# A start in another order: attention and a channel mix on one TensorE

## The chip, the core and the metric

The program runs on one core of a Trainium2 chip. A core has TensorE (PE: matmuls, with a separate queue of weight loads, PEld), VectorE (DVE), ScalarE (ACT), GpSimd (POOL) and SyncE (SP), which issues the transfers here; each works through its own instructions in a fixed order and waits at semaphores for the others. The metric is the device time of one execution in microseconds (us). Another execution, taken by the hardware profiler, left the profile and the trace that are read below.

## The reference

Attention with pooled keys and values, then a channel mix on its output, in float32; the three weights reach the program in 64 bits:

```python
# q, k, v: [8, 8, 576, 64];  w_k: [512, 1024], w_v: [1024, 512], w_r: [512, 512]
k_p = k.reshape(B, H, 72, 8, D).mean(axis=3)      # v_p likewise
scores = scale * np.matmul(q, k_p.transpose(0, 1, 3, 2))
attn = np.exp(scores - np.max(scores, axis=-1, keepdims=True))
attn = attn / (np.sum(attn, axis=-1, keepdims=True) + 1e-09)
x = np.matmul(attn, v_p)                          # then [B, S, H * D] = [8, 576, 512]
x_prev = ...                                      # x, one token later, 0 at a batch's first
xk = mu_k * x + (1.0 - mu_k) * x_prev
xr = mu_r * x + (1.0 - mu_r) * x_prev
k = np.maximum(xk @ w_k, 0.0)
v = k * k @ w_v
return 1.0 / (1.0 + np.exp(-(xr @ w_r))) * v
```

## The kernel before, in words

**Tiles and stages.** The 8 x 576 tokens are 36 tiles of 128 and 12 chunks of 384. A tile has its scores (L524, all heads, 576 columns in a pair of PSUM banks `sc`), its softmax on VectorE and ScalarE (maximum L535, `e` L542 or L549 and after, sum L556, 1/sum L559 and L562), the division by the sum (`px` L566 for the last 8 keys, `pm` L572 for the first 64) and transposes (`pth` L589, of `pm`; `pr` copies L618 and L620, L622, and their transposes L628). A chunk has four attention products (L671, into `bank`), their mix with the token before (L678 on ScalarE, small copies through `carry` L687 and L689 on GpSimd, L696 on VectorE), eight hidden groups (`x_k @ w_k`, L740, then relu and square, `sh`), three gates (L789) and three mixing groups (L821). Chunk 0 works in full float32, where one matmul of the program is two records of PE in the trace. Later chunks split each operand in a high and a low fp32r part (`xkh`, `xkl`, `sh`, `sl`, `w_k` high and low, by L408 and L411) and take three matmuls of such parts for one.

**Sums and weights.** The pooled sum over 8 rows of k (`keys`), v (`values`) and of v's last 8 keys (`last_values`) goes for batches 0 and 1 through PE, as eight matmuls with the identity (L429, `SUMMED_ON_PE`); for later ones it is three halvings (L418), k's on VectorE, v's on GpSimd. k0 to k3, v0 to v3, r0 and r1 are the parts of the first two batches. Each of the 20 weight blocks is turned from 64-bit to float32 words by `convert`: |x| on ScalarE, then four VectorE instructions (L374, L376, L381, L386) through one of two places `tmp`; `split` makes the two parts when chunk 0 has used the block, the low one on VectorE or GpSimd by the table `LOW_BY`.

**What sets the order.** Nothing is reordered at run time. A planner, `Order`, writes the program: each piece of work is a generator that yields what it needs (`need`), the place it takes (`take`) or the next instruction with its engine and estimated length; pieces have a due time (`order.add(due, ...)`, from `FIRST`, `PER_TOKEN`, `tile_due`), and the planner hands out instructions by due times, estimated lengths and the estimated delay between engines (`LATENCY`). Its results are one fixed order per engine. `LOADS` is the order of the first transfers on SP's queue; `stage` has three places for raw k and v, `qs` two for q, `sc` one pair of banks, `bank` and `mm` three banks each. `BY_HEAD` names the tiles whose exponentials are eight small ScalarE instructions with the sum beside them, `COPIES_ON_ACT` the number of tiles whose `pr` copies are on ScalarE.

Of the kernel before, what the change touches and what calls it, by code (L numbers as in the profile page):

```python
# [173 lines left out]
def attention_then_channel_mix(  # L174
# [122 lines left out]
    def load_constants():  # L297
        yield "sp", 0.6, False
        nc.sync.dma_start(out=mask_sb, in_=mask)
        order.fetched("mask", 2)  # L300
        yield "sp", 0.6, False
        nc.sync.dma_start(out=mu_sb, in_=mu)
        order.fetched("mu", 2)
# [614 lines left out]
```

## Time and profile before

| what | us |
|---|---|
| median of 3 runs (660.5 to 662.31) | 661.78 |
| the profiled execution | 657.92 |
| its span in the trace | 656.1 |
| first attention product begins | 33.46 |
| first hidden matmul of chunk 1 begins | 109.86 |
| first gate matmul of chunk 1 begins | 134.31 |
| last mixing matmul ends | 652.05 |

All times in rows of the trace are us from the start of the span. The four moments in the middle cut the span in stages: the first sums and softmaxes; chunk 0's products, hidden groups, gates and mixing groups, with the conversion of all weights; chunk 1's hidden groups; and the other chunks. In a row of the timeline stand the start, the duration, the engine, the line of the kernel, the operation, out<-in with its shape, and, in brackets, the idle time before it and what ended that; "x8" behind a row is eight instructions of one group in a row. In a row of groups stand the busy time in all, the mean of one in ns, and the idle time before them. In a row of windows stand a stretch and its length, and for each engine the busy time and the instructions.

### The profile page before, as it was taken

How to read it: one execution, taken by the hardware profiler on the slowest of the kernel's cores; microseconds unless marked ns; L12 is line 12 of the kernel's file. 1: busy time of each engine (PE TensorE's matmuls, PEld its weight loads, DVE VectorE, ACT ScalarE, POOL GpSimd, SP SyncE). 2: the span in 40 equal slices, each digit the busy share in tenths (PEclk: the TensorE clock that was granted, in tenths of full speed). 3: DMA queues.
4: the chain of work that ended last, by engine and by line, in shares of the span. 5: the costliest groups of instructions: out<-in, count | busy, mean ns of one | idle time of the engine just before them, and what ended most of it. 6: DMA issues, size and time to landing. Idle time of an engine off the chain costs nothing.

```text
span 656.1 us, 9196 instructions
## 1 busy us (share of the span) xinstructions
PE 631.1 (96%) x3328; PEld 546.8 (83%) x3328; DVE 415.8 (63%) x797; ACT 335.7 (51%) x713; POOL 211.9 (32%) x329
## 2 busy tenths in 40 slices
PE   6699989899999999999999999999999999999997
PEld 6555646888988988988978998998988998998986
DVE  2789966885776667854884657754784654653421
ACT  3766447575456455554464446455365445454420
POOL 1211036636147017505344206604443303302200
PEclk9989999999999999999999999999999999999999
DMA  7893014012240115101411105101321101000001
GB/s 255 279 378 145 0 49 151 2 50 71 93 133 33 48 43 183 33 26 39 169 40 49 33 16 199 43 17 48 139 71 40 42 17 32 33 1 29 20 1 48
DMA packets 34989, 50.93 MB, mean 78 GB/s; under 512 B 6528, under 2 KB 22912, under 8 KB 34944
## 3 DMA queue, kind: packets, MB, share of 16 engines
q1 hardware_dynamic: 34944, 50.35, 22.7%
q8 instruction: 26, 0.43, 0.3%
q14 instruction: 19, 0.16, 0.1%
HBM read 40.90 MB, written 9.44 MB: 77 GB/s over the span
## 4 chain that ended last, share of the span: by engine, by line
PE 71%; DVE 16%; issue 5%; POOL 3%; ACT 3%; DMA 1%; POOLq 0%; ACTq 0%; DVEq 0%
PE mm L821 28%; PE mm L740 20%; PE mm L789 10%; PE bank L671 5%; PE sc L524 4%; PE bank L589 2%; DVE rk L757 2%; DVE sl L765 2%; PE mm L429 1%; DVE stage L418 1%; DVE pr L620 1%; DVE tmp L381 1%; DVE vbd_l L472 1%; DVE mx L535 1%; POOL pm L572 1%
## 5 line engine op out<-in xcount | busy, mean ns | idle before, releaser
L740 PE MATMUL mm<-xkh,w_k 128*128 128x384 f32 x704 | 182.2, 339 | 1.5 <-DVE rk L757 1.5
L821 PE MATMUL mm<-w_v,sh 128*128 128x512 f32 x528 | 171.0, 392 | 0.0
L740 PEld LDWEIGHTS mm<-xkh,w_k 128*128 128x128 f32 x704 | 125.3, 188 | 2.8 <-DVE rk L757 1.7
L740 PE MATMUL mm<-xkl,w_k 128*128 128x384 f32 x352 | 118.3, 336 | 1.6 <-POOL xkl L714 1.5
L821 PEld LDWEIGHTS mm<-w_v,sh 128*128 128x128 f32 x528 | 99.2, 188 | 19.5
L821 PE MATMUL mm<-w_v,sl 128*128 128x512 f32 x264 | 102.9, 390 | 0.0
L566 POOL TENSOR_TENSOR px<-e,sm 128x64 f32<-128x64 f32 x36 | 12.1, 337 | 264.5 <-DVE sm L562 255.4
L789 PE MATMUL mm<-w_r,xrh 128*128 128x512 f32 x264 | 86.7, 398 | 0.1
L763 ACT CAST sh<-rk 128x384 fp32r<-128x384 f32 x88 | 45.2, 514 | 65.9 <-DVE rk L757 65.8
L678 ACT ACTIVATE t<-bank,om_sb 128x384 f32<-128x384 f32 x96 | 49.3, 580 | 46.4 <-PE bank L671 46.0
L696 DVE SCALAR_TENSOR_TENSOR xm<-bank,mu_sb,t 128x384 f32<-128x384 f32 x88 | 50.3, 613 | 30.8 <-POOL t L689 13.2
L830 DVE TENSOR_TENSOR rs<-mm,rs 128x512 f32<-128x512 f32 x36 | 24.8, 690 | 69.0 <-PE mm L821 69.0
L740 PEld LDWEIGHTS mm<-xkl,w_k 128*128 128x128 f32 x352 | 66.1, 188 | 2.5 <-POOL xkl L714 2.5
L765 DVE TENSOR_TENSOR sl<-rk,sh 128x384 fp32r<-128x384 f32 x88 | 50.2, 575 | 22.1 <-ACT sh L763 22.1
L757 DVE SCALAR_TENSOR_TENSOR rk<-mm,rk 128x384 f32<-128x384 f32 x88 | 48.5, 552 | 17.7 <-ACT rk L750 17.4
L789 PEld LDWEIGHTS mm<-w_r,xrh 128*128 128x128 f32 x264 | 49.6, 188 | 10.2 <-DVE rk L757 0.4
L714 POOL TENSOR_TENSOR xkl<-xm,xkh 128x384 fp32r<-128x384 f32 x44 | 45.2, 1027 | 39.4 <-ACT xkh L712 39.0
L821 PEld LDWEIGHTS mm<-w_v,sl 128*128 128x128 f32 x264 | 49.7, 188 | 9.0
L418 POOL TENSOR_TENSOR stage<-stage 128x512 f32<-128x512 f32 (+5 forms) x54 | 46.9, 873 | 29.7 <-DMA stage<-in_vm 18.5
L750 ACT ACTIVATE rk<-mm 128x384 f32<-128x384 f32 x88 | 42.9, 487 | 25.3 <-PE mm L740 24.3
L789 PE MATMUL mm<-w_r,xrl 128*128 128x512 f32 x132 | 51.4, 390 | 0.0
L714 POOL TENSOR_TENSOR xrl<-xm,xrh 128x384 fp32r<-128x384 f32 x44 | 45.1, 1024 | 1.2 <-ACT xrh L712 1.2
(102 smaller groups left out, 975.4 us busy)
## 6 DMA issues: line engine op xcount, KB each, us to landing
stage<-in_kT SPq DMA_DIRECT2D x16, 576.0 KB, 5.0
out<-rs SPq DMA_DIRECT2D x36, 256.0 KB, 2.0
qs<-in_qT SPq DMA_DIRECT2D x32, 256.0 KB, 3.2
stage<-in_vm SPq DMA_DIRECT2D x16, 512.0 KB, 4.9
got_wk<-in_w_k SPq DMA_DIRECT2D x8, 512.0 KB, 6.4
got_wv<-in_w_v SPq DMA_DIRECT2D x8, 512.0 KB, 10.3
stage<-in_vr SPq DMA_DIRECT2D x8, 384.0 KB, 3.8
got_wr<-in_w_r SPq DMA_DIRECT2D x4, 512.0 KB, 6.1
```

The lines of the kernel that those rows point to most:

```text
L418: nc_eng.tensor_tensor(out=st[:, :, :w], in0=st[:, :, :w], in1=st[:, :, w:2 * w], op=ALU.add)
L671: nc.tensor.matmul(out=xp[:, o], lhsT=v, rhs=p, start=(q == 0), stop=(q == len(terms) - 1))
L678: nc.scalar.activation(out=t[:, m, 1:n + 1], in_=xp, func=AF.Copy, scale=om_sb[:, m, g:g + 1])
L696: nc.vector.scalar_tensor_tensor(out=xm[:, :n], in0=xp, scalar=mu_sb[:, m, g:g + 1], in1=t[:, m, :n], op0=ALU.mult, op1=ALU.add,)
L714: nc.gpsimd.tensor_tensor(out=lo, in0=xm[:, :n], in1=hi, op=ALU.subtract)
L740: nc.tensor.matmul(out=hp, lhsT=w[:, o], rhs=x[:, ct, :n], start=(ct == 0 and k == 0), stop=(ct == NCT - 1 and k == len(terms) - 1),)
L750: nc.scalar.activation(out=rk[:, :n], in_=hp, func=AF.Relu)
L757: nc.vector.scalar_tensor_tensor(out=rk[:, :n], in0=hp, scalar=0.0, in1=rk[:, :n], op0=ALU.max, op1=ALU.mult)
L763: nc.scalar.copy(out=sh[:, :n], in_=rk[:, :n])
L765: nc.vector.tensor_tensor(out=operand(f"sl{jt}", c)[:, :n], in0=rk[:, :n], in1=sh[:, :n], op=ALU.subtract)
L789: nc.tensor.matmul(out=bank, lhsT=x[:, ct, o], rhs=w, start=(ct == 0 and k == 0), stop=(ct == NCT - 1 and k == len(terms) - 1),)
L821: nc.tensor.matmul(out=bank, lhsT=s[:, o], rhs=w, start=(jt == 0 and k == 0), stop=(jt == NJT - 1 and k == len(terms) - 1),)
```

## The change

It edits the part of the program that deals with the first two batches, and some numbers of the planner:

- Four matmuls on zeros (`warm`) stand first on PE.
- `LOADS` has another order; the masks and `mu` go in it ("c0").
- `SUMMED_ON_PE` becomes a table `SUM_BY`: k0, v0, v1 and r0 stay on PE ("t"); k1, k2 and k3 are halved on VectorE ("v"); v2, v3 and r1 on GpSimd ("g").
- The divisions of tiles 0 to 3 go from GpSimd to VectorE (`NORM_BY`), all `pr` copies from ScalarE to VectorE (`COPIES_ON_ACT`), one low part of w_v from VectorE to GpSimd (`LOW_BY`), and tile 1's exponentials from by-head to whole rows (`BY_HEAD`).
- Tile 1's scores go to two `mm` banks (`BESIDE`) in place of the `sc` pair; maximum and difference are then two instructions of half the width each.
- Raw k and v may also be loaded in the places that chunk 1's `sl`, `ptl` and `xrl` take later (`early`), which then wait until the raw data was used; `sl` and `sh` become one tile each of eight blocks; `qs` has three places.
- Due times (`EARLIER`, `SECOND`, `FIRST`), `SPARE` and `LATENCY` of the planner change.

Its lines move the numbers: L429 becomes L474, L418 L463, L524 L582, L535 L595, L566 L632, L572 L638, L589 L657, L618 L686, L620 L688, L628 L696, L671 L739, L687 L762, L689 L764, L740 L815, L789 L864, L821 L896; L374, L376, L381, L386 become L419, L421, L426, L431, and L411 L456.

```diff
...
-    "k0 k1 q0 wk0 v0 v1 r0 q1 wk1 q2 wk2 k2 k3 wk3 v2 v3 r1 wk4 q3 wk5 q4 wk6 wk7 "
-    "wr0 q5 wr1 wr2 wr3 wv0 wv1 wv2 wv3 wv4 wv5 wv6 wv7"
+    "k0 k1 q0 q1 wk0 v0 v1 wk1 c0 q2 r0 wk2 wk3 k3 wk4 v3 v2 q3 wk5 r1 k2 wk6 wk7 q4 wr0 q5 wr1 wr2 "
+    "wr3 wv0 wv1 wv2 wv3 wv4 wv5 wv6 wv7 "
...
-SUMMED_ON_PE = (0, 1)
-LOW_BY = {"k": "gvgvgvgv", "r": "gvgv", "v": "gvgvgvgv"}
-BY_HEAD = (0, 1, 2)
+SUM_BY = {
+    "k0": "t", "k1": "v", "v0": "t", "v1": "t", "r0": "t", "k2": "v", "k3": "v", "v2": "g", "v3": "g",
+    "r1": "g",
+}
+NORM_BY = {0: "v", 1: "v", 2: "v", 3: "v"}
+WARMING = 4
+LOW_BY = {"k": "gvgvgvgv", "r": "gvgv", "v": "gvgggvgv"}
+BY_HEAD = (0, 2)
+BESIDE = (1,)
-COPIES_ON_ACT = 6
-SPARE = 2.5
-FIRST = 27.0
+COPIES_ON_ACT = 0
+EARLIER = {
+    "transposed_rest 6": 3.3, "hidden 2 5": -0.6, "convert r 1": -1.2, "mixed 0 1": -1.6,
...
+}
+SPARE = 3.0
+SECOND = 24.0
+FIRST = 22.0
...
-    LATENCY = {"pe": 0.185, "dve": 0.095, "act": 0.105, "pool": 0.065, "sp": 0.0}
+    LATENCY = {"pe": 0.195, "dve": 0.13, "act": 0.14, "pool": 0.1, "sp": 0.0}
...
-    slots("qs", 2, [P, NPAIR, P])
+    slots("qs", 3, [P, NPAIR, P])
     slots("stage", 3, [P, 2 * POOL * KEYS])
+    early = {}
+    for tag, n in (("sl", 2), ("ptl", 1), ("xrl", 1)):
+        t = sb.tile([P, n, 2 * POOL * KEYS], F32, name=f"early_{tag}", tag=tag)
+        for i in range(n):
+            got = t[:, i]
+            early[id(got)] = (tag, i), got
+            order.give("stage", got)
...
+    def warm():
+        zeros = yield take("tmp")
+        yield "dve", 0.5, False
+        nc.vector.memset(zeros, 0.0)
+        bank = yield take("bank")
+        for _ in range(WARMING):
+            yield "pe", 0.86, False
+            nc.tensor.matmul(out=bank[:, :256], lhsT=zeros[:, :P], rhs=zeros[:, :256], start=True, stop=True)
...
-    def sums(st, cols, b, eng):
+    def sums(st, cols, eng):
         raw, v = st
-        if b in SUMMED_ON_PE:
+        if eng == "t":
             bank, o = yield from summed(v, cols)
-            order.give("stage", raw)
+            done_with("stage", raw)
             return "mm", bank, o
         for n in (4, 2, 1):
-            yield (dve if eng is nc.vector else pool)(2 * n * cols)
-            halve(eng, v, cols, n)
+            yield (dve if eng == "v" else pool)(2 * n * cols)
+            halve(nc.vector if eng == "v" else nc.gpsimd, v, cols, n)
...
-        kind, raw, o = yield from sums(held.pop(("k", 2 * b + p)), KEYS, b, nc.vector)
+        kind, raw, o = yield from sums(held.pop(("k", 2 * b + p)), KEYS, SUM_BY.get(f"k{2 * b + p}", "v"))
...
-        sc = yield take("sc")
+        if i in BESIDE:
+            pair = [(yield take("mm")), (yield take("mm"))]
...
-        yield "pool", 0.24, True
-        nc.gpsimd.tensor_tensor(
+        v = NORM_BY.get(i, "g") == "v"
+        eng = nc.vector if v else nc.gpsimd
+        yield dve(8 * KR) if v else ("pool", 0.24, True)
+        eng.tensor_tensor(
             out=px, in0=e[:, :, :, KM:], in1=sm.broadcast_to([P, 2, 4, KR]), op=ALU.mult
         )
...
         yield need(("pm", i), *([("attended", c - 1)] if c else []))
+        if c == 1:
+            yield need(("early", "ptl", 0))
...
-            yield need(("gated", c - 1))
+            yield need(("gated", c - 1), ("early", "xrl", 0))
...
-            yield need(("mixed", c - 1))
-        sh = operand(f"sh{jt}", c)
+            yield need(("mixed", c - 1), ("early", "sl", 0), ("early", "sl", 1))
+        sh = operand("sh", c)[:, jt]
...
```

The tables move instructions, as three places show. PE at the start of the program, up to the first attention product, before (`mm` holds a pooled sum, `sc` scores, `bank` a transpose or a product):

```order
L429 MATMUL mm_112<-stage_105,ident 128x144 x8
L429 MATMUL mm_113<-stage_106,ident 128x144 x8
L524 MATMUL sc_108<-kbd_69,qs_103 128x144 x4
L429 MATMUL mm_114<-stage_107,ident 128x128 x8
L429 MATMUL mm_112<-stage_105,ident 128x128 x8
L429 MATMUL mm_113<-stage_106,ident 96x128 x8
L524 MATMUL sc_108<-kbd_69,qs_104 128x144 x4
L589 MATMUL bank_109<-ident,pm_90 128x128 x4
L628 MATMUL bank_110<-ident,pr_94 96x128 x2
L429 MATMUL mm_112<-stage_107,ident 128x144 x8
L524 MATMUL sc_108<-kbd_69,qs_103 128x144 x4
L429 MATMUL mm_113<-stage_106,ident 128x128 x8
```

The same place now:

```order
L337 MATMUL bank_113<-tmp_101 128x256 x4
L474 MATMUL mm_116<-stage_106,ident 128x144 x8
L582 MATMUL sc_112<-kbd_69,qs_103 128x144 x4
L582 MATMUL mm_118<-kbd_69,qs_104 128x144 x2
L582 MATMUL mm_116<-kbd_69,qs_104 128x144 x2
L474 MATMUL mm_118<-stage_108,ident 128x128 x4
L582 MATMUL sc_112<-kbd_69,qs_105 128x144 x4
L657 MATMUL bank_114<-ident,pm_90 128x128 x4
L696 MATMUL bank_115<-ident,pr_94 96x128 x2
L474 MATMUL mm_118<-stage_108,ident 128x128 x4
L474 MATMUL mm_116<-early_sl,ident 128x128 x4
L657 MATMUL bank_113<-ident,pm_91 128x128 x4
```

In front stand the zeros; one k's sum is left there, the second tile's scores follow the first's at once in two `mm` banks, and the sums of v1 and r0 stand between the transposes.

PE from chunk 0's last hidden group (L740) through its gates (L789), before:

```order
L740 MATMUL mm_112<-xkh_364,got_wk_342 128x384 x4
L429 MATMUL mm_113<-stage_107,ident 128x128 x4
L789 MATMUL mm_112<-got_wr_346,xrh_366 128x512
L789 MATMUL mm_112<-got_wr_373,xrh_366 128x512
L789 MATMUL mm_112<-got_wr_378,xrh_366 128x512
L789 MATMUL mm_112<-got_wr_381,xrh_366 128x512
L429 MATMUL mm_113<-stage_107,ident 128x128 x4
L429 MATMUL mm_114<-stage_106,ident 96x128 x8
L789 MATMUL mm_112<-got_wr_346,xrh_366 128x512
L789 MATMUL mm_112<-got_wr_373,xrh_366 128x512
```

and now, where the same lines are L815 and L864:

```order
L815 MATMUL mm_116<-xkh_354,got_wk_270 128x384 x4
L864 MATMUL mm_117<-got_wr_291,xrh_358 128x512
L864 MATMUL mm_117<-got_wr_304,xrh_358 128x512
L864 MATMUL mm_118<-got_wr_291,xrh_358 128x512
L864 MATMUL mm_117<-got_wr_315,xrh_358 128x512
L864 MATMUL mm_118<-got_wr_304,xrh_358 128x512
L864 MATMUL mm_118<-got_wr_315,xrh_358 128x512
L864 MATMUL mm_117<-got_wr_323,xrh_358 128x512
L864 MATMUL mm_118<-got_wr_323,xrh_358 128x512
```

The pooled sums of batch 1 are gone from between the gates, and the first two gates now run side by side, block by block of w_r.

VectorE at the conversions of w_r (`got_wr`), before:

```order
L374 TENSOR_SCALAR tmp1_102<-tmp1_102 128x512
L376 TENSOR_SCALAR tmp1_102<-tmp1_102 128x512
L381 SCALAR_TENSOR_TENSOR tmp1_102<-got_wr1_373,tmp1_102 128x512
L386 SCALAR_TENSOR_TENSOR got_wr1_373<-got_wr1_373,tmp1_102 128x512
L374 TENSOR_SCALAR tmp0_101<-tmp0_101 128x512
L376 TENSOR_SCALAR tmp0_101<-tmp0_101 128x512
L381 SCALAR_TENSOR_TENSOR tmp0_101<-got_wr2_378,tmp0_101 128x512
L386 SCALAR_TENSOR_TENSOR got_wr2_378<-got_wr2_378,tmp0_101 128x512
```

and now:

```order
L419 TENSOR_SCALAR tmp1_102<-tmp1_102 128x512
L419 TENSOR_SCALAR tmp0_101<-tmp0_101 128x512
L421 TENSOR_SCALAR tmp1_102<-tmp1_102 128x512
L421 TENSOR_SCALAR tmp0_101<-tmp0_101 128x512
L426 SCALAR_TENSOR_TENSOR tmp1_102<-got_wr0_291,tmp1_102 128x512
L426 SCALAR_TENSOR_TENSOR tmp0_101<-got_wr1_304,tmp0_101 128x512
L431 SCALAR_TENSOR_TENSOR got_wr0_291<-got_wr0_291,tmp1_102 128x512
L431 SCALAR_TENSOR_TENSOR got_wr1_304<-got_wr1_304,tmp0_101 128x512
```

Each instruction stood right behind the one whose result it takes; now two blocks go in turns. GpSimd from chunk 0's mix (`t` and `carry` belong to it) to the splits of w_k, before:

```order
L687 COPY carry<-t_81 128x2
L689 MEMSET t_81 128x2
L687 COPY carry<-t_82 128x2
L689 MEMSET t_82 128x2
L411 TENSOR_TENSOR w_k_445<-got_wk_126,w_k_445 128x512
L566 TENSOR_TENSOR px_93<-e_89,sm_99 128x64
L572 TENSOR_TENSOR pm_91<-e_89,sm_99 128x512
L411 TENSOR_TENSOR w_k_630<-got_wk_174,w_k_630 128x512
L411 TENSOR_TENSOR w_k_648<-got_wk_311,w_k_648 128x512
```

and now:

```order
L762 COPY carry<-t_81 128x2
L764 MEMSET t_81 128x2
L463 TENSOR_TENSOR early_xrl<-early_xrl 128x2x128
L463 TENSOR_TENSOR early_xrl<-early_xrl 128x2x64
L463 TENSOR_TENSOR stage_107<-stage_107 96x2x256
L762 COPY carry<-t_82 128x2
L764 MEMSET t_82 128x2
L463 TENSOR_TENSOR stage_107<-stage_107 96x2x128
L463 TENSOR_TENSOR stage_107<-stage_107 96x2x64
L456 TENSOR_TENSOR w_k_431<-got_wk_136,w_k_431 128x512
L456 TENSOR_TENSOR w_k_551<-got_wk_161,w_k_551 128x512
L456 TENSOR_TENSOR w_k_589<-got_wk_174,w_k_589 128x512
```

The divisions (L566, L572) are no longer there, and the halvings of v2, v3 and r1 (L463) stand between the small copies.

More of the change, by code (lines that the diff above doesn't have):

```diff
@@ L295, in constants, with complements @@
         order.make(("values clear", 1))
[L297 to L303, printed above, removed]
+    def warm():
[6 more added lines that the diff above has]
+            nc.tensor.matmul(out=bank[:, :256], lhsT=zeros[:, :P], rhs=zeros[:, :256], start=True, stop=True)
+        order.give("bank", bank)
+        order.give("tmp", zeros)
+    def complements():
         yield need("mu")
@@ L329, in load @@
     def load(kind, i):
+        if kind == "c":
+            yield "sp", 1.0, False
+            nc.sync.dma_start(out=mask_sb, in_=mask)
+            nc.sync.dma_start(out=mu_sb, in_=mu)
+            order.fetched("mask", 2)
+            order.fetched("mu", 2)
+            return
         if kind == "q":
@@ L454, in keys @@
             nc.scalar.copy(out=kbd[b % 2][r, gs, h2 * KEYS:(h2 + 1) * KEYS], in_=o[r])
-        order.give(kind, raw)
+        done_with(kind, raw)
         order.make(("keys", b, p))
@@ L461, in values @@
         yield need(("v", 2 * b + p), ("attended", last_chunk[b - 2]) if b > 1 else ("values clear", b))
-        kind, raw, o = yield from sums(held.pop(("v", 2 * b + p)), D, b, nc.gpsimd)
+        if not b:
+            yield need(*[("scored", i) for i in BESIDE])
+        kind, raw, o = yield from sums(held.pop(("v", 2 * b + p)), D, SUM_BY.get(f"v{2 * b + p}", "g"))
         gs = slice(2 * p, 2 * p + 2)
@@ L474, in values @@
                 )
-        order.give(kind, raw)
+        done_with(kind, raw)
         order.make(("values", b, p))
@@ L491, in last_values @@
         yield need(("r", b), "mask", *([("attended", last_chunk[b - 2])] if b > 1 else []))
-        kind, raw, o = yield from sums(held.pop(("r", b)), D, b, nc.gpsimd)
+        kind, raw, o = yield from sums(held.pop(("r", b)), D, SUM_BY.get(f"r{b}", "g"))
         vq = yield take("vq")
@@ L498, in last_values @@
         nc.vector.tensor_tensor(out=vq[lo], in0=o[lo], in1=vq[lo], op=ALU.subtract)
-        order.give(kind, raw)
+        done_with(kind, raw)
         yield "dve", 0.67, True
@@ L509, in last_values, with scored @@
         order.make(("rest", b))
+    def scored(sc, pair):
+        for t in pair or [sc]:
+            order.give("mm" if pair else "sc", t)
     def softmax(i):
@@ L516, in softmax @@
         yield need(("q", i), *[("keys", b, p) for b, *_ in parts for p in range(2)])
-        sc = yield take("sc")
+        pair = None
+        if i in BESIDE:
+            pair = [(yield take("mm")), (yield take("mm"))]
+            sc = None
+            halves = [t.rearrange("p (a n) -> p a n", a=1) for t in pair]
+        else:
+            sc = yield take("sc")
+            halves = [sc[:, a:a + 1] for a in range(2)]
         order.make(("scoring", i))
@@ L529, in softmax @@
         order.make(("scored", i))
-        sv = sc[:, :, :4 * KEYS].rearrange("p a (h k) -> p a h k", k=KEYS)
+        whole = [sc] if pair is None else halves
+        svs = [t[:, :, :4 * KEYS].rearrange("p a (h k) -> p a h k", k=KEYS) for t in whole]
         mx = yield take("mx")
@@ L675, in attended, with shifted @@
             order.make(("attended", c))
-        yield "act", 2 * act(n)[1] + 0.12, False
-        for m in range(2):
+        yield from shifted(c, g, (0, 1), bank, t, True)
+    def shifted(c, g, ms, bank, t, last):
+        n = CHUNKS[c]
+        whole = c in WHOLE
+        xp = bank[:, :n]
+        yield "act", len(ms) * (act(n)[1] + 0.05), False
+        for m in ms:
             nc.scalar.activation(
@@ L699, in attended @@
             )
-            if m:
+            if m == ms[-1] and last:
                 order.give("t", t)
```

78 lines of the change are left out of this document (46 added, 32 removed), and 2 rows, old and new, of the table EARLIER.

## The prediction

> **What bounds the kernel now.** I read the page's first part, then the busy time by stage, cut where the first attention product (33.46), the first matmul of chunk 1 (109.86) and its first gate matmul (134.31) begin.
>
> ```profile
> span 656.1 us, 9196 instructions
> PE 631.1 (96%) x3328; PEld 546.8 (83%) x3328; DVE 415.8 (63%) x797; ACT 335.7 (51%) x713; POOL 211.9 (32%) x329
> ```
> ```profile
> 0.00:33.46 33.46, 21.89 (x155) 20.14 (x155) 16.95 (x39) 17.96 (x78) 6.53 (x15) 0.99 0.80 267
> 33.46:109.86 76.40, 72.83 (x287) 43.61 (x287) 61.74 (x113) 43.82 (x89) 16.26 (x28) 0.98 0.35 129
> 109.86:134.31 24.45, 21.34 (x126) 19.72 (x125) 19.93 (x38) 15.20 (x35) 14.06 (x22) 1.00 0.21 78
> 134.31:652.05 517.74, 515.05 (x2767) 463.33 (x2765) 316.48 (x608) 258.75 (x515) 175.01 (x265) 1.00 0.18 58
> ```
>
> After each stretch and its length stand the busy times of PE, PEld, DVE, ACT and POOL, the granted clock and the DMA. From 134.31 on PE waits 2.7 us in 518, on work that the change leaves alone. What can be had lies ahead: PE idle is 11.6 in the first row, 3.6 in the second, 3.1 in the third. In the first, VectorE is idle too (16.5 of 33.46): neither bounds it, the chain of waits does:
>
> ```profile
> 4.95 6.25 PE mm L429 x32
> ...
> 27.85 2.32 ACT e L542 x15
> ...
> 31.08 1.01 POOL pm L572
> ...
> 33.46 3.40 PE bank L671 x6
> ```
>
> Sums, three softmaxes one after another (one pair of score banks), GpSimd's division, then the products. In the second row PE is nearly full and VectorE has 61.7 of 76.4.
>
> **The change, part by part.** *First scores.*
>
> ```profile
> 4.95 6.24 PE L429 MATMUL mm<-stage,ident 128*128 128x144 f32 x32 [4.95 <-DMA stage<-in_kT]
> 9.16 0.56 ACT L454 COPY kbd<-mm 64x144 f32<-64x144 f32 x2 [6.34 <-PE mm L429]
> 12.63 0.76 DVE L535 TENSOR_REDUCE mx<-sc 128x8 f32<-128x576 f32 x1 [0.56 <-PE sc L524]
> ```
> ```profile
> stage<-in_kT SPq DMA_DIRECT2D x16, 576.0 KB, 5.0
> ```
>
> Half of the 32 records are k0's: done at about 9.1, 0.26 us each; the other half takes 2.1, or 0.13 each. PE is slow for its first 4 us. The four matmuls on zeros (8 records of 256 columns, 0.26 x 256/144 = 0.46 each, 3.7 us) run from about 1.5 to 5.2, when k0 is there; its sum at the fast rate ends at 7.4, its copies (0.56) at 8.0. k1 lands at about 1.2 + 5.0 = 6.2 and VectorE adds it up in some 1.5 beside that (three halvings, the largest 0.75, quoted below); copies to 8.6, two more score matmuls, and the first maximum starts at 9.4, not 12.6. That is 3.2 earlier. The zeros themselves are free: they run before any load has landed, and without that cover would cost their 3.7. In SP's queue q1 now goes ahead of wk0, so that the first weights land one transfer later; that wait is counted below.
>
> [...]
>
> *To the first attention product.* The second tile's scores no longer wait for the pair of banks, and k1's sum, the divisions (PE and GpSimd before) and the `pr` copies (ScalarE before) stand on VectorE. From the first maximum to the last `vbd_r` product VectorE has 45 instructions, 16.8 us of durations. They overlap, as these rows show:
>
> ```profile
> 50.34 0.42 DVE L374 TENSOR_SCALAR tmp<-tmp 128x512 f32<-128x512 f32 x1
> 50.80 0.43 DVE L376 TENSOR_SCALAR tmp<-tmp 128x512 int32<-128x512 int32 x1
> 51.26 0.69 DVE L381 SCALAR_TENSOR_TENSOR tmp<-got_wr,tmp 128x512 int32<-128x512 int32 x1
> 51.99 0.69 DVE L386 SCALAR_TENSOR_TENSOR got_wr<-got_wr,tmp 128x512 int32<-128x512 int32 x1
> 52.60 0.42 DVE L374 TENSOR_SCALAR tmp<-tmp 128x512 f32<-128x512 f32 x1
> ```
>
> One that uses the result right ahead starts 0.03 after its end, one that doesn't 0.08 before it (52.60 against 52.68). 39 of the 45 are of the second kind: 13.8. With 2 us of waits (0.8 for wk0 and its |x|, 0.5 for `vq`, small ones) they end at 9.4 + 13.8 + 2.0 = 25.3; tile 2's probabilities are there by then: 25.4 for 33.46, **-8.1**. Bounds: 23.3 without waits, 28.3 without overlap. The places lent for loads bring new waits (chunk 1's `ptl`, `xrl` and `sl` may be written only when the stage in their place is copied): by the order, the last such copy, of k3's sum, stands behind the conversions of w_k, and the first `ptl` behind those of w_r, some 10 us later, so they cost nothing; if k3's copy were late, VectorE's conversions of w_v would stand behind `ptl`.
>
> *PE's work from there to chunk 1.* The sums of k2, k3, v2, v3 and r1 leave PE; three of them stand behind 33.46:
>
> ```profile
> 60.12 1.05 PE L429 MATMUL mm<-stage,ident 128*128 128x128 f32 x8
> ...
> 65.61 2.80 PE L429 MATMUL mm<-stage,ident 128*128 128x128 f32 x24
> ...
> 75.12 2.12 PE L429 MATMUL mm<-stage,ident 128*128 128x144 f32 x16
> ```
>
> **-6.0**, all on PE's path. And PE ran at half clock:
>
> ```profile
> 32.13 0.66 PE L589 MATMUL bank<-ident,pm 128*128 128x128 f32 x4 [3.32 <-POOL pm L572]
> 33.46 1.65 PE L671 MATMUL bank<-pth,vbd_w 128*128 128x384 f32 x2 [0.46 <-ACT pth L597]
> ...
> 36.68 1.14 PE L524 MATMUL sc<-kbd,qs 128*128 128x144 f32 x8
> ...
> 39.78 0.81 PE L671 MATMUL bank<-pth,vbd_w 128*128 128x384 f32 x2
> ...
> ```
> ```profile
> 33.50:34.00 0.50, 0.50 (x1) 0.50 1.16 393
> 36.00:36.50 0.50, 0.50 (x3) 0.50 1.16 339
> ```
>
> After 3.3 idle us the clock stood at 0.50 to 36.5: two groups took 3.2 us where the last takes 0.82. Now v1's and r0's sums stand between the transposes just ahead of the products, so I expect no such gap there: **-1.6** (0 if there is one). PE's own work is then 72.83 - 6.0 - 1.6 = 65.2: without a wait chunk 1 would begin at 25.4 + 65.2 = 90.6.
>
> *What PE waits for.* VectorE must finish the 20 conversions by then, and now has 172 instructions from the first maximum to the last of w_v, where it had 119: halvings, divisions and copies come in, four `w_k` splits and chunk 1's softmaxes move ahead.
>
> ```profile
> L535 DVE TENSOR_REDUCE mx<-sc 128x8 f32<-128x576 f32 x36 | 27.0, 750 | 5.3 <-PE sc L524 5.2
> L549 DVE TENSOR_TENSOR e<-sc,mx 128x576 f32<-128x576 f32 x33 | 24.9, 755 | 0.8
> ...
> L411 DVE TENSOR_TENSOR w_k<-got_wk,w_k 128x512 fp32r<-128x512 f32 x4 | 2.7, 686 | 3.3 <-ACT w_k L408 3.3
> L696 DVE SCALAR_TENSOR_TENSOR xkh<-bank,mu_sb,t 128x384 f32<-128x384 f32 x4 | 2.5, 616 | 1.3 <-POOL t L689 1.2
> ```
> ```profile
> 132.99 0.75 DVE L418 TENSOR_TENSOR stage<-stage 128x576 f32<-128x576 f32 x1
> ```
>
> 20 conversions x 2.24 (the four rows of L374 to L386) = 44.8; reductions 10 x 0.75 and 2 halves, 8.3; 6 of 576 elements, 4.5; 11 of 512, 7.5; 8 mixes, 4.9; 76 small ones, 12.9: 82.9, against 60.4 before. Only 16 use the result right ahead (61 before), since conversions now go in pairs: 82.9 + 16 x 0.02 - 156 x 0.08 = 70.8, of which 57.0 lie behind 25.3. To it comes GpSimd:
>
> ```profile
> 47.29 1.40 POOL L411 TENSOR_TENSOR w_k<-got_wk,w_k 128x512 fp32r<-128x512 f32 x1 [4.51 <-ACT w_k L408]
> 47.59 1.39 DVE L376 TENSOR_SCALAR tmp<-tmp 128x512 int32<-128x512 int32 x1
> ...
> 84.45 1.26 POOL L411 TENSOR_TENSOR w_k<-got_wk,w_k 128x512 fp32r<-128x512 f32 x1 [19.03 <-ACT w_k L408]
> ...
> 119.66 2.60 POOL L418 TENSOR_TENSOR stage<-stage 128x512 f32<-128x512 f32 x3
> ```
>
> The 0.43 of L376 became 1.39 beside GpSimd's split: it waited that out. In this stretch GpSimd gets three sums (7.8), four splits (5.1), two divisions (1.3 each, with `px`) and small copies (1.2): 16.7. Queued behind those sums are the carry copies, for which the mixes and so PE wait. The cost lies between 0 (all beside instructions that read PSUM, or waits) and 16.7; I take half, 8.4, since about a quarter of VectorE's time there is such reading and it waits for PE too. The last conversion ends at 25.3 + 57.0 + 8.4 = 90.7. Behind it PE still has four mixing matmuls and two groups of products, 4 x 0.88 + 2 x 0.89 = 5.3, so 96.0:
>
> ```profile
> 77.73 7.03 PE L821 MATMUL mm<-got_wv,sh 128*128 128x512 f32 x16
> ...
> 105.75 0.27 PE L671 MATMUL bank<-pth,vbd_h 128*128 128x192 f32 x1
> ...
> 106.64 1.17 PE L524 MATMUL sc<-kbd,qs 128*128 128x144 f32 x8
> ```
>
> (7.03 is eight matmuls; a group of eight began at 105.75 and ended at 106.64.) The 96.0 are 5.4 above PE's own 90.6, and as the two also wait on each other in turn (scores for the maximum, probabilities for `ptl`) I take 7.5 idle us in PE, 98.1 in all, for 3.6 before: **+3.9**.
>
> *The rest.* Chunk 1's matmuls and all later ones are the same, softmax pieces a few places earlier or later. Splits of w_r that now fall behind chunk 1's start and four of w_v in a row on GpSimd may cost PE 3 us; a second and third score bank's worth of work to do meanwhile may save most of the 3.1: 0, between -3 and +3.
>
> Sum: -8.1 - 6.0 - 1.6 + 3.9 = **-11.8**. The profiled execution took 657.92 (1.8 around its span) and would take 646.1; the median shown is 661.78, 3.9 higher, so **650.0**.
>
> **Rivals.** *PE never waits* (VectorE's overlap as above, GpSimd beside it): 90.6, 7.5 better, 642.5. For it: VectorE alone would be done at 82.3. Against it: strict queues, and 3.6 us of waits already before.
>
> *VectorE is the bound, without the overlap*: 28.3 + 66.1 + 8.4 + 5.3 = 108.1 for 109.86, 660.0. PE's idle time then takes the place of all that was saved. For it: +22.5 us on an engine that was 81% busy. Against it: the overlap stands in each row pair above.
>
> *Slower: the same with GpSimd's 16.7 in full*: 116.4, 6.5 later, 668.3. It decides from where VectorE needs over 109.86 - 5.3 - 9.4 = 95.2 us from the first maximum to the last conversion (forecast 81.3). [...]
>
> *The zeros don't raise the clock*: k0's sum takes 4.15, 2 us later: 652.0, inside the forecast.
>
> **How the numbers follow.** Forecast, 645.5 to 656: 0.62. PE without waits: 0.07. VectorE as the bound, 656 to 663.8: 0.23, about half above 659.8. Slower: 0.08. A difference of 0.3% (2.0 us) is about what a measurement tells from none: faster 0.62 + 0.07 + 0.12 = 0.81, same 0.11, slower 0.08. The range 645.5 to 661.5 leaves out 0.07 below and some 0.13 above.
>
> **What would show it.** First maximum at 9.4, first product at 25.4 at full clock, no L429 row behind it, the first hidden matmul of chunk 1 at 98, idle PE of about 7.5 between, VectorE nearly full from 28 to 90. I am wrong if VectorE's rows stand end to end, if many last over 1 us beside GpSimd's, or if the stretch after chunk 1 grows.

## The result and the profile after

The changed kernel takes 636.91 us (median of 4 runs, 635.93 to 637.27), the kernel before beside it 661.14 (659.11 to 662.31): ratio 0.9634, 95% interval 0.9607 to 0.9662. The forecast was 650.0, in a range from 645.5 to 661.5. Faster was right; the gain is twice the one forecast, and the time lies below the range. Medians here and below leave out three executions that ran far longer (714.87 us of before_spare30, 1266.7 of after_spare25, 891.79 of same_norms_pool, the profiled one there). The profiled execution took 637.27 and its span 635.5, which is 20.6 less than the 656.1 before. By the stages of the prediction:

| stage (us) | before | forecast | after |
|---|---|---|---|
| to the first attention product | 33.46 | 25.4 | 25.24 |
| from there to the first hidden matmul of chunk 1 | 76.40 | 72.7 | 69.94 |
| chunk 1's hidden groups | 24.45 | 24.45 (with the next row -3 to +3) | 22.19 |
| to the end of the last matmul | 517.74 | 517.74 | 514.38 |
| from there to the end of the span | 4.05 | 4.05 | 3.75 |

The first part of the page of the changed kernel, and its windows for the first four stages (columns as before: a stretch, its length, busy us of PE, PEld, DVE, ACT and POOL, granted clock, DMA share, GB/s):

```profile
span 635.5 us, 9032 instructions
PE 621.6 (98%) x3240; PEld 537.8 (85%) x3240; DVE 413.7 (65%) x829; ACT 334.2 (53%) x688; POOL 215.2 (34%) x331
```
```profile
0.00:25.24 25.24, 20.04 (x115) 17.80 (x115) 17.05 (x51) 13.74 (x53) 2.15 (x9) 0.93 0.95 335
25.24:95.18 69.94, 65.99 (x238) 36.64 (x239) 68.26 (x138) 43.90 (x87) 24.34 (x36) 1.00 0.47 167
95.18:117.37 22.19, 21.23 (x126) 19.96 (x125) 20.15 (x44) 14.58 (x32) 15.62 (x23) 1.00 0.07 25
117.37:631.75 514.38, 514.30 (x2765) 463.41 (x2764) 307.58 (x600) 261.96 (x518) 173.08 (x265) 1.00 0.18 58
```

PE's idle time is length less PE's busy time: 5.2, 3.95, 0.96 and 0.08, where it was 11.6, 3.6, 3.1 and 2.7. In the second row VectorE is busy for 68.3 of 69.9, and PE for 66.0 of the same 69.9: both are nearly full at once. PE's waits there, from the view of waits (in all, times, longest):

```profile
PE mm L815 <- DVE xkh L771: 2.1, 2, 1.1
PE mm L864 <- DVE got_wr L431: 1.3, 1, 1.3
PE bank L739 <- ACT pth L665: 0.5, 1, 0.5
PE bank L696 <- DVE pr L690: 0.4, 1, 0.4
PE mm L896 <- DVE got_wv L431: 0.2, 1, 0.2
```

They are small and early; the last conversion of a weight (last row of the second fence below, from the timeline of VectorE) ends at 90.2, and the matmul that uses it begins within 0.1 us of that, so PE came to it just in time. The timeline of PE, then of VectorE, and a row of ScalarE:

```profile
1.45 3.78 PE L337 MATMUL bank<-tmp 128*128 128x256 f32 x8 [1.45 <-DVE tmp L333]
5.03 3.36 PE L474 MATMUL mm<-stage,ident 128*128 128x144 f32 x16
...
15.32 2.26 PE L582 MATMUL sc<-kbd,qs 128*128 128x144 f32 x8
...
25.24 0.91 PE L739 MATMUL bank<-pth,vbd_w 128*128 128x384 f32 x2 [0.49 <-ACT pth L665]
```
```profile
10.48 0.76 DVE L595 TENSOR_REDUCE mx<-sc 128x8 f32<-128x576 f32 x1 [2.80 <-PE sc L582]
...
17.61 0.76 DVE L595 TENSOR_REDUCE mx<-sc 128x8 f32<-128x576 f32 x1 [0.47 <-PE sc L582]
...
41.18 1.56 DVE L519 TENSOR_TENSOR vbd_l<-stage,vbd_h 64x128 fp32r<-64x128 f32 x2
...
43.38 0.60 DVE L519 TENSOR_TENSOR vbd_l<-early_xrl,vbd_h 64x128 fp32r<-64x128 f32 x2
...
89.53 0.68 DVE L431 SCALAR_TENSOR_TENSOR got_wv<-got_wv,tmp 128x512 int32<-128x512 int32 x1
```
```profile
24.61 0.58 ACT L665 COPY pth<-bank 128x512 f32<-128x512 f32 x1
```

The first product starts at full clock (0.91 for two records, before 1.65). The scores at 15.32 took 2.26 where such a group takes 1.15: a stretch at half clock (granted clock 0.50 from 15 to 17). VectorE waited 0.47 us for them with the third tile's maximum (17.61). From 18.2 on ScalarE works without a gap, up to the copy of `pth` at 24.61 for which the first product waits its 0.49.

### The profile page after: what moved, and what is told of

It is laid out like the page before. It is cut to its first block, busy times and chain, and to the rows that moved or that the text cites. A ratio compares the mean times of both kernels' runs of the same rounds, so it can differ in the third digit from the quotient of the medians.

```text
span 635.5 us, 9032 instructions
## 1 busy us (share of the span) xinstructions
PE 621.6 (98%) x3240; PEld 537.8 (85%) x3240; DVE 413.7 (65%) x829; ACT 334.2 (53%) x688; POOL 215.2 (34%) x331
## 4 chain that ended last, share of the span: by engine, by line
PE 81%; DVE 8%; DMA 6%; POOL 2%; issue 1%; ACT 1%; SPq 1%; ACTq 0%; POOLq 0%; DVEq 0%
PE mm L896 28%; PE mm L815 26%; PE mm L864 15%; PE bank L739 5%; PE sc L582 4%; PE bank L657 2%; DMA qs<-in_qT 2%; DMA early_xrl<-in_vm 1%; DMA got_wk<-in_w_k 1%; DMA got_wv<-in_w_v 1%; PE bank L696 1%; DVE tmp L426 1%; DVE tmp L419 1%; DVE pr L688 1%; POOL xrl L789 1%
## 5 line engine op out<-in xcount | busy, mean ns | idle before, releaser
L815 PE MATMUL mm<-xkh,w_k 128*128 128x384 f32 x704 | 182.3, 339 | 0.3 <-ACT xkh L787 0.3
L896 PE MATMUL mm<-w_v,sh 128*128 128x512 f32 x528 | 170.8, 392 | 0.0
L815 PEld LDWEIGHTS mm<-xkh,w_k 128*128 128x128 f32 x704 | 125.6, 188 | 1.9 <-issue 0.6
L815 PE MATMUL mm<-xkl,w_k 128*128 128x384 f32 x352 | 118.2, 336 | 0.7 <-POOL xkl L789 0.7
L896 PEld LDWEIGHTS mm<-w_v,sh 128*128 128x128 f32 x528 | 99.2, 188 | 19.8 <-issue 0.2
L896 PE MATMUL mm<-w_v,sl 128*128 128x512 f32 x264 | 103.0, 390 | 0.0
L632 POOL TENSOR_TENSOR px<-e,sm 128x64 f32<-128x64 f32 x32 | 10.8, 339 | 225.0 <-DVE sm L626 224.8
L864 PE MATMUL mm<-w_r,xrh 128*128 128x512 f32 x264 | 84.9, 394 | 0.0
L840 DVE TENSOR_TENSOR sl<-rk,sh 128x384 fp32r<-128x384 f32 x88 | 53.3, 609 | 25.5 <-ACT sh L838 25.4
L815 PEld LDWEIGHTS mm<-xkl,w_k 128*128 128x128 f32 x352 | 66.1, 188 | 1.3 <-POOL xkl L789 1.3
L864 PEld LDWEIGHTS mm<-w_r,xrh 128*128 128x128 f32 x264 | 49.6, 188 | 10.0
L789 POOL TENSOR_TENSOR xkl<-xm,xkh 128x384 fp32r<-128x384 f32 x44 | 44.8, 1021 | 38.2 <-ACT xkh L787 37.9
L896 PEld LDWEIGHTS mm<-w_v,sl 128*128 128x128 f32 x264 | 49.7, 188 | 9.0
L463 POOL TENSOR_TENSOR stage<-stage 128x512 f32<-128x512 f32 (+5 forms) x60 | 50.7, 852 | 13.7 <-ACT rk L825 5.9
L864 PE MATMUL mm<-w_r,xrl 128*128 128x512 f32 x132 | 51.4, 389 | 0.0
L595 DVE TENSOR_REDUCE mx<-sc 128x8 f32<-128x576 f32 x35 | 26.3, 751 | 32.6 <-PE sc L582 32.6
```

The source lines that it names most:

```text
L463: nc_eng.tensor_tensor(out=st[:, :, :w], in0=st[:, :, :w], in1=st[:, :, w:2 * w], op=ALU.add)
L789: nc.gpsimd.tensor_tensor(out=lo, in0=xm[:, :n], in1=hi, op=ALU.subtract)
L815: nc.tensor.matmul(out=hp, lhsT=w[:, o], rhs=x[:, ct, :n], start=(ct == 0 and k == 0), stop=(ct == NCT - 1 and k == len(terms) - 1),)
L840: nc.vector.tensor_tensor(out=operand("sl", c)[:, jt, :n], in0=rk[:, :n], in1=sh[:, :n], op=ALU.subtract)
L864: nc.tensor.matmul(out=bank, lhsT=x[:, ct, o], rhs=w, start=(ct == 0 and k == 0), stop=(ct == NCT - 1 and k == len(terms) - 1),)
L896: nc.tensor.matmul(out=bank, lhsT=s[:, o], rhs=w, start=(jt == 0 and k == 0), stop=(jt == NJT - 1 and k == len(terms) - 1),)
```

## The experiments

The table gives the median and the stages of the profiled execution, in us; the last stage here goes to the end of the span. A name with "same" keeps the planner's order. The rows come from several measurements; the control, same_order, was measured together with same_norms_again alone.

| kernel | median | to first product | to chunk 1 | its hidden groups | rest |
|---|---|---|---|---|---|
| before | 661.14 | 33.46 | 76.40 | 24.45 | 521.79 |
| before_again | 659.37 | 35.39 | 78.80 | 24.46 | 519.65 |
| before_filled | 657.93 | 34.58 | 76.14 | 24.45 | 521.33 |
| before_spare30 | 657.2 | 35.86 | 76.39 | 24.44 | 517.81 |
| before_late | 656.36 | 33.75 | 76.70 | 24.41 | 517.94 |
| before_sums | 661.92 | 35.62 | 82.97 | 18.23 | 520.58 |
| before_norms | 661.74 | 35.24 | 77.92 | 27.53 | 519.11 |
| before_same_norms | 659.67 | 34.55 | 78.38 | 24.43 | 521.54 |
| after | 636.91 | 25.24 | 69.94 | 22.19 | 518.13 |
| same_order (control) | 637.44 | 25.40 | 69.90 | 22.19 | 517.81 |
| after_spare25 | 638.0 | 25.91 | 69.89 | 22.14 | 518.86 |
| after_no_late | 638.32 | 24.57 | 70.10 | 22.19 | 519.34 |
| after_no_warm | 637.17 | 25.06 | 70.20 | 22.16 | 518.58 |
| after_sums_pe | 649.41 | 24.67 | 76.13 | 29.14 | 517.46 |
| after_norms_pool | 659.06 | 26.03 | 70.63 | 23.31 | 536.13 |
| after_no_early | 649.11 | 27.86 | 81.70 | 19.38 | 517.86 |
| same_norms_pool, same_norms_again | 638.0, 638.39 | 24.95 | 71.52 | 22.19 | 517.74 |
| same_sums_vector | 639.34 | 26.80 | 71.91 | 22.14 | 518.35 |
| same_sums_pe | 648.19 | 25.26 | 82.83 | 22.18 | 517.73 |

### Why before varies, and its profile was short

before_again is the kernel before, unchanged.

> The kernel before, once more. Its one profiled execution took 657.92, its timed ones 659.11 to 662.31. Theory A (an execution of this program varies by 3 to 4 us, and the profiled one was a short one): this profile takes 659 to 662 and its span shows longer waits of PE or a longer stretch of lower granted clock than 656.1 had. Theory B (a profiled execution of this program is always shorter than a timed one): 657.9 again, timed 660 to 662.

Its executions went from 656.81 to 661.44, the profiled one took 660.15. Theory A holds. Windows on PE of this execution (length, PE busy, granted clock, DMA share, GB/s):

```profile
20.00:23.00 3.00, 1.05 (x6) 1.00 1.02 409
23.50:26.00 2.50, 2.50 (x12) 0.50 0.40 159
33.50:40.00 6.50, 6.15 (x18) 0.50 1.07 354
98.50:101.50 3.00, 3.00 (x14) 0.50 0.24 90
```

The clock stood at about 0.50 for 3.4, 6.8 and 3.4 us. PE was busy for 13.1 us of these, so some 6.5 us were lost (an estimate: half of that time); in the execution that the prediction read it was 3.4 us once, 1.5 lost. Still the two executions differ by 2.2 us only: behind chunk 1, PE waited for `pm` 2.4 us in the one that the prediction read and 0.8 in this one (2.1 and 2.3 in before_filled and before_same_norms), so these waits vary from execution to execution too. The first stretch follows three short gaps, not one long one: PE was busy for 1.05 of the 3 us ahead. Over 83 later executions of the kernel before the median is 659.15 (655.8 to 663.1); the 39 with a mean granted clock up to 0.9925 average 660.6, the 18 above 0.9955 average 657.8. The execution profiled before the prediction, at 0.996, was of the second kind. The executions of before that stand beside the result (661.14) were high ones: against 659.15 the change gains 22 us and not 24.

before_filled puts matmuls on zeros into PE's gaps.

```diff
+    FILL = {("scored", 1): 2, ("main", 0): 2, ("side", 0): 2, ("side", 1): 7}
...
+            for _ in range(FILL[what, i]):
+                nc.tensor.matmul(out=bank[:, :256], lhsT=zeros[:, :P], rhs=zeros, start=True, stop=True)
```

> The kernel before with 13 matmuls on zeros (256 columns) put into PE's idle gaps from 19 to 33 us, 7 of them in the 3.3 us ahead of the third tile's transposes; nothing reads them. Theory A (the idle gaps cost TensorE's clock, half speed for 3.4 or 6.8 us at a time, 1.7 or 3.4 us lost, and how often it happens makes executions differ by 6 us): granted clock 1.00 from 12 to 96, first product no later than 33.5 with its first groups at 0.8 in place of 1.65, time 2 to 4 below that of before, executions closer together. Theory B (the clock's share is small): the same time, or 1 us more for the matmuls.

The clock was 1.00 in every window from 10 to 105, and the first products took 0.91 and 0.81. Yet the median, 657.93, is within the noise of before (ratio 0.999, 0.9961 to 1.002), and the seven executions with a mean clock of 0.999 or more still spread from 655.19 to 659.26. What was won in clock was mostly lost again: the first product came at 34.58, after a wait of PE of 1.2 us for raw k, and a wait of 0.8 for a q stands behind it; why these came is open. So the clock is part of before's spread, not all of it, and filling gaps won nothing clear of the noise here: theory B.

### The planner's numbers behind chunk 1

before_spare30 and after_spare25 change one number, the reserve: how long after a softmax's result the planner puts PE's work on it, from chunk 2 on.

```diff
-SPARE = 2.5
+SPARE = 3.0
```

> The kernel before with only the planner's reserve SPARE at 3.0 in place of 2.5 (PE's work for a softmax's result is planned 3.0 us after the result for chunks 2 and later). Theory A (the 2.4 us that PE waited for pm at 341 and 491 go by the larger reserve): the stretch from chunk 1's first gate matmul to the last mixing matmul is 515.2 in place of 517.7, the time 2.4 lower, ratio 0.996. Theory B (they go because the earlier start moves the later softmaxes): the same waits, the same time within 0.5.

> The changed kernel with SPARE back at 2.5. Theory A (the reserve takes PE's waits behind chunk 1 away): 2 to 3 us of waits for pm come back behind 117, 639 to 640. Theory B (the order of the start does): no wait there, 636.9 within 0.5.

In before_spare30 no wait of PE is left behind chunk 1, 517.81 for that stage where three executions with 2.5 have 521.3 to 521.8 and one 519.65; ratio 0.9958 (0.9936 to 0.9979). Theory A. In the changed kernel the number matters less: without the larger reserve one wait of 0.5 us comes back, 0.7 in the stage and some 1 in the time, which lies between the two theories. The two waits that the prediction took as untouched were these, from the view of waits of the kernel before, 134.31 to 652.05:

```profile
PE bank L589 <- POOL pm L572: 2.4, 2, 1.5
```

before_late adds six of the due times to the larger reserve, after_no_late takes the six and the reserve away.

```diff
+EARLIER = {"transposed_rest 6": 3.3, "transposed_rest 8": 9.6, "hidden 2 5": -0.6, "hidden 2 6": 3.9,
+    "hidden 2 3": -1.7, "hidden 1 5": -1.3,
+}
```

> The kernel before with the numbers of the change that name chunks 1 and 2 only: the six due times of EARLIER for tiles 6 and 8 and for hidden groups of chunks 1 and 2, and SPARE 3.0. Theory A (what was won behind the first hidden matmul of chunk 1, 2.3 in its hidden groups and 3.7 behind them, comes from these numbers): the two stretches take 22.2 and 518.1 in place of 24.45 and 521.8, the time is 5 to 6 lower than before, ratio 0.992. Theory B (it comes from the new order of the start, which brings chunk 1's softmaxes and parts earlier): no more than with SPARE alone, ratio 0.996.

> The changed kernel without the six due times for chunks 1 and 2 and with SPARE 2.5, the start's five due times left. Theory A (these numbers won 6 us): chunk 1's hidden groups take 24.4 for 22.2 and the rest 521 for 518.1, 642 to 643. Theory B (the start's order won them): 637 to 638.5, as with SPARE 2.5 alone (638.3).

Theory B both times: chunk 1's hidden groups stay at 24.41 with these numbers and at 22.19 without them. So the 2.3 us there come from the rest of the change, which orders the start anew. The 3.4 behind cannot be given to one side: in the kernel before the reserve alone takes these waits away (517.81), and in the changed kernel most of them stay away without it (518.86 and 519.34). The waits in chunk 1's hidden groups, first before, then after:

```profile
PE mm L740 <- POOL xkl L714: 1.5, 2, 1.0
PE mm L740 <- DVE rk L757: 1.5, 1, 1.5
```
```profile
PE mm L815 <- POOL xkl L789: 0.7, 2, 0.5
PE mm L815 <- ACT xkh L787: 0.3, 1, 0.3
```

And VectorE's timeline there, before:

```profile
118.73 2.24 DVE L620 CAST pr<-px 128x64 fp32r<-128x64 f32 x2 [1.95 <-POOL px L566]
120.89 1.01 DVE L757 SCALAR_TENSOR_TENSOR rk<-mm,rk 128x384 f32<-128x384 f32 x2
```

The two `pr` copies waited 1.95 us for a division that stood on GpSimd behind four splits of chunk 1's mix, then took 2.24 beside GpSimd, and `rk`, for which PE waited 1.5, stood behind them. In the new order the first two `rk` stand ahead of the next tile's `pr` copies, and that wait is gone; VectorE's timeline, after:

```profile
104.62 1.01 DVE L832 SCALAR_TENSOR_TENSOR rk<-mm,rk 128x384 f32<-128x384 f32 x2
...
108.37 0.49 DVE L688 CAST pr<-px 128x64 fp32r<-128x64 f32 x2
```

### The zeros

```diff
-    order.add(-30, warm())
```

> The changed kernel without the four matmuls on zeros. Theory A (they bring full rate to k0's sum only near its end, 3.36 for 4.15 us, and VectorE's work behind the first maximum passes it on): first maximum at 11.3 in place of 10.5, first product at 26.0 in place of 25.2, 637.7. Theory B (as the prediction sized them, 2 us): 639. Theory C (the start has slack behind the first maximum): first product at 25.2, 636.9 within 0.3.

First maximum at 11.19, first product at 25.06, 637.17: theory C. Without zeros k0's sum took 4.18 for 3.36, and the first maximum came 0.7 us later. But PE kept its full clock from 10 to 20 us, so VectorE did not wait for the third tile's scores: that tile's maximum came at 17.76 for 17.61. ScalarE, again without a gap from that tile's exponentials on, copied `pth` at 24.43 for 24.61. What the zeros won at the start, the half clock behind took back.

### Parts undone or done alone, the planner free

after_sums_pe, after_norms_pool and after_no_early each undo one part (the last drops the waits for the lent places too); before_sums and before_norms do one part in the kernel before. In this order:

```diff
-    "k0": "t", "k1": "v", "v0": "t", "v1": "t", "r0": "t", "k2": "v", "k3": "v", "v2": "g", "v3": "g",
-    "r1": "g",
+    "k0": "t", "k1": "v", "v0": "t", "v1": "t", "r0": "t", "k2": "t", "k3": "t", "v2": "t", "v3": "t",
+    "r1": "t",
...
-NORM_BY = {0: "v", 1: "v", 2: "v", 3: "v"}
+NORM_BY = {}
...
-    for tag, n in (("sl", 2), ("ptl", 1), ("xrl", 1)):
+    for tag, n in ():
...
-SUMMED_ON_PE = (0, 1)
+SUMMED_ON_PE = (0,)
...
+        v = i < 4
+        eng = nc.vector if v else nc.gpsimd
+        yield dve(8 * KM) if v else ("pool", 1.0, True)
```

> The changed kernel with the sums of k2, k3, v2, v3 and r1 back on PE (five sums, 9.1 us of records at 0.13 to 0.14 each, of which the prediction counted three behind the first product at 6.0). Theory A (PE's own work bounds the stretch from 25 to 95, so what is taken off PE is won in full): 6 us more, 643. Theory B (VectorE, busy 68.3 of 69.9 there, bounds it; its three halvings of two k and the share of GpSimd's 7.8 that it waited out would be gone): 0 to 2 us more, 637 to 639.

> The changed kernel with the divisions of tiles 0 to 3 back on GpSimd. Theory A (the chain of the start is shorter by them): first product 2 to 3 us later, at 27.5 to 28, chunk 1 as much later, 640. Theory B (VectorE bounds the start and the stretch behind it, and gets 3.6 us of work less): no later, 637 or less.

> The changed kernel without the places lent by chunk 1's parts: raw k and v have the three stage places alone. Theory A (the lent places bring the loads of v1, r0, k3, v3 and r1 ahead, and the sums and softmaxes with them): loads wait for places, first product 1 to 3 us later or chunk 1 later, 639 to 642. Theory B (loads are early enough without them): 637 within 0.6.

> The kernel before with only batch 1's pooled sums off PE (k2 and k3 halved on VectorE; v2, v3 and r1 on GpSimd; all of batch 0 stays). Theory A (PE's own 6.0 us behind the first product is what this part is worth, as the prediction had it): 653, ratio 0.991. Theory B (it is worth 12 us, as undoing it in the changed kernel cost, since it also gets chunk 1's softmaxes ahead and shortens chunk 1's hidden groups): 647, ratio 0.981, and the hidden groups of chunk 1 take 22 in place of 24.45. Theory C (VectorE and GpSimd give it back, as they are full without the rest of the change): 657 or more.

> The kernel before with only the divisions of tiles 0 to 3 on VectorE in place of GpSimd. Theory A (each division stands in the chain to the first product and saves 0.9 us there, 1.8 on GpSimd for 0.9 on VectorE, and the 2.3 us that PE waits for tile 3's pm go too): first product at 31, time 3 to 5 lower, 655. Theory B (VectorE's own queue gives it back): within 1 us of before.

Undone, the parts cost 12.5, 22 and 12 us, twice the whole gain; alone, two of them make the kernel before slower (ratios 1.0036 and 1.0041, both intervals above 1). None of the theories for the three parts undone, nor for before_norms, expected this. The table shows where: after_norms_pool loses 18 of its 22 behind chunk 1's hidden groups, where no division of these tiles stands. Its waits of PE from 117 to 250:

```profile
PE mm L815 <- DVE rk L832: 4.7, 2, 4.5
PE mm L896 <- DVE w_v L456: 2.5, 1, 2.5
PE mm L896 <- POOL w_v L456: 2.1, 2, 1.8
PE mm L864 <- DVE w_r L456: 1.7, 1, 1.7
```

Splits of w_r and w_v, and an `rk`, come too late in the order that the planner made from another start. These waits are 11.5 of the 18 us; the rest is busy time of PE (521.0 for 514.3), with 3.4 and 6.8 us at half clock. In before_norms the divisions took 0.69 in place of 1.0, but stood behind conversions in VectorE's queue, and PE waited 5.4 us for them:

```profile
PE bank L591 <- DVE pm L574: 5.4, 3, 4.1
```

In before_sums PE's matmuls waited 5.4 us for conversions of w_v and 1.8 for w_r: theory C by its time. Chunk 1's hidden groups were 6.2 shorter, as theory B had it, but the stage ahead was 6.6 longer and the first product came 2.2 later; PE also ran at half clock from 22 to 39 us, so the conversions are not the whole of it. In after_no_early PE waited 5.1 us for a conversion of w_v and 3.4 for nothing that the profile shows, and ran at half clock for 13.7 us; the lent places were not tried with the order kept.

### The order kept

Here the sequence of the planner's choices is written into the kernel and replayed, so that an edit changes an operation's engine and not the order. The edits are those of NORM_BY, SUM_BY and the divisions above; same_sums_vector sets v2, v3 and r1 to "v".

```diff
+            k = next(k for k, n in enumerate(self.picks) if n in now)
+            t = now[self.picks.pop(k)]
```

> The changed kernel itself, its planner's choices written into the kernel: the same instructions in the same order, as the control on the chip of the later runs. Theory: 636.9 within 0.6 as on the first chip, and the stretches of its trace within 1 us. If it is 1 or more above that, the prices of 1.7 (divisions) and 2.4 (sums on VectorE) shrink by as much.

> The changed kernel with the divisions of tiles 0 to 3 back on GpSimd, every step of the planner kept in the place that it has in the changed kernel (the sequence of its choices is written into the kernel). Theory A (of the 22 us that undoing this part cost, nearly all came from the new order that the planner then made): first product 0.5 to 1.5 us later, chunk 1 up to 1 more as GpSimd's split and sums wait, 637.5 to 639.5. Theory B (the part itself is worth 22 us): 655 or more.

> The divisions back on GpSimd with the order kept, once more for its trace, which the first run did not give. Theory A (the price of 1.7 lies ahead of the first product): first product 0.8 to 1.5 later than in the control, the stretches behind it as there. Theory B (it lies in the stretch behind, where GpSimd's divisions hold VectorE up): first product within 0.5 of the control, chunk 1's first hidden group 1.5 later.

The control took 637.44, the divisions on GpSimd 638.0 and 638.39: they are worth about 1 us (theory A of the first, by its time), and about 21 of the 22 belonged to the order. The trace of the second puts the price behind the first product (71.52 for 69.90): theory B by its place. A stretch at half clock from 40 to 44 us, behind a wait of 2.3 us for a mix, makes most of it.

> The changed kernel with v2, v3 and r1 halved on VectorE in place of GpSimd, the order kept. VectorE gets nine halvings, 3 x (0.68 + 0.4 + 0.3) = 4.1 us, GpSimd loses 7.8; carry copies no longer queue behind the sums. Theory A (VectorE is the bound from 25 to 90 and waits out about 1 us of these sums only): chunk 1 begins 3 us later, 640. [...]

VectorE was busy 70.35 in place of 68.21 in the second stage, which took 71.91: of the 4.1 us put on it half came through, and 639.34 is 1.9 above the control. Theory A, a little less than sized. (The profiled execution, the slowest of the four, began chunk 1 3.4 later; 1.4 of that stood ahead of the first product, with 6.8 us at half clock.)

> The changed kernel with batch 1's five sums back on PE, the order kept as far as the mm banks allow (8 matmuls each in the places of the halvings). Theory A (PE and VectorE are both full from 25 to 95, so that PE's 9.1 us are added, less what VectorE's 3 us give): 6 to 9 more, 643 to 646; the rest of the 12.5 that undoing this part cost came from the planner's new order. Theory B (the sums on PE cost 12 in any order): 649.

Between the theories: 648.19, 10.8 above the control; in the profiled execution, 649.83, it stands all in the second stage (82.83, 12.9 more). PE was busy 77.56 there, 11.6 more: 10.4 of sums, the rest a stretch of 3.4 us at half clock; its idle time grew by 1.3. The stages behind are as in the changed kernel. VectorE, with 65.46 of 82.83, did not bound it.

> The kernel before with the divisions of tiles 0 to 3 on VectorE, every step kept in its place in the order of before. Theory A (each of the three divisions ahead of the first product is then 0.9 us shorter, and tile 3's 2.3 us wait goes): first product near 31.5, 3 to 4 us less, 655 to 656; with the planner's new order it was 2.6 slower. Theory B (the part gives nothing without the rest): within 1.5 of before.

659.67 (ratio 0.9998, 0.9978 to 1.0019): theory B. In the order of before, PE waited as long for the divisions on VectorE (4.2 us) as it had for GpSimd, since conversions stood ahead of them.

## Why the prediction was too high

Three terms failed: the 0 for the stages behind chunk 1's start, the offset from span to median, and the 2.1 us of waiting added to the bounds. The start's sum came out right.

**First product, -8.1.** Right in sum (-8.2), in part by luck. The zeros did less: PE came to its fast rate at 7.4 us, inside k0's sum, which took 3.36, not the 2.1 assumed, and the first maximum came at 10.48, not 9.4. From there to the first product 14.8 us passed, where 13.8 + 2.0 were forecast, so that 1.1 too little and 1.0 too much cancelled. VectorE was nearly full on that way, as the prediction had it (busy for 13.5 of the 14.3 us from 10.48 to 24.75). But what the first product waited for stood at the end of ScalarE's queue, and the prediction took ScalarE's part as done by then. As after_no_warm shows, the zeros' share was none.

**Sums off PE, -6.0, and half clock, -1.6.** PE's busy time of the second stage fell by 6.8 (72.83 to 65.99) for 7.6. The part itself is worth 10.8 with the order kept: all five sums would stand behind the first product there, and cost clock and waits besides.

**PE's idle time, +3.9.** It was +0.4. The bounds were near: the last conversion ended at 90.2 (forecast 90.7), and chunk 1 began 5.0 later (5.3). The step that failed here is the 2.1 us added for PE and VectorE waiting on each other; with the 96.0 from the bounds, the stage would have come within 0.8 of the measured 95.18. Of GpSimd's work I took half, 8.4 us, as lost to VectorE, an estimate between two ends that the trace of before has: L376 took 1.39 for 0.43 beside the split at 47.29, while L535 and L549, which read `sc`, kept their 0.75 and 0.76 at 87.61 and 88.39 beside the split at 87.82. In the changed kernel, rows that are longer than their like (1.56 beside 0.60 above) add up to about 6.

**The rest, 0.** This is the largest miss: -2.3 in chunk 1's hidden groups and -3.4 behind them, together outside the -3 to +3 allowed. The prediction called the 2.7 us of waits behind 134.31 "work that the change leaves alone". The reserve, which the change raises from 2.5 to 3.0, is alone enough to take them away (before_spare30), and the new order takes most of them away without it (after_spare25). The waits in chunk 1 hung on the order in which its softmaxes and splits share VectorE and GpSimd (after_no_late against before_late, and the rows above).

**The offset, +3.9.** I took the distance of the profiled execution from the shown median over to the changed kernel. It belongs to the kernel before, whose executions differ, in part by the clock lost on its gaps (1.5 us in the one profiled, 6.5 in another). Its median is 659.15 over 83, so 2.6 of the 3.9 came from three long executions and 1.2 from a short profiled one. The changed kernel's executions spread over 1.3 us, and its profiled one stands 0.4 above its median. Of the 13.1 us by which the forecast was too high, this is 4.2, the rest of the trace 5.9 (with 0.3 at the end, which no run explains), the idle time and PE's work 2.8, the first product 0.2.

**The rivals.** The nearest was PE without waits, 642.5, at 0.07; PE's waits behind the first product were in fact those of before, 4 us. VectorE as the bound without overlap, at 0.23, and GpSimd's work in full did not come; where one part was done alone, in before_sums, PE did wait 7.2 us for conversions.

What is open: with the order kept, the sums (10.8) and the divisions (about 1) are half of the gain, and the order of loads, the lent places, the second tile's score banks and the `pr` copies were not priced so. Which part of the start's new order shortens chunk 1's hidden groups was not separated from the others; nor is it known why the waits for `pm`, and the executions of the kernel before beyond their clock, differ.

## What to carry to other kernels

With a planner that orders work by estimates, parts of a change can be worth nothing alone and much together, as here; undoing a part with the planner free prices the new order, so keep the order when an operation is to be priced. A reserve or a due time is part of the change in every stage that it reaches: read the waits of all stages with it in mind. Before a distance between a profiled execution and the median is carried over, ask what makes executions differ, and whether the changed kernel still has it.
